# Infini-attention with MLP: inverse sums spread by four transfers, and head outputs weighed into the tile they arrive in

## The chip, the cores and the metric

The kernel runs on one core of one Trainium2 chip. The time is the device time of one execution in microseconds (us), and a kernel's time is the median of its runs. Five engines work side by side, each through its own queue of instructions: TensorE (PE in the profile; its weight loads are PEld), VectorE (DVE), ScalarE (ACT), GpSimd (POOL) and SyncE (SP). SP issues nearly all DMA transfers of the part that is spoken of here. "Granted clock" is the share of TensorE's full clock that the throttle allowed.

## The reference

A sequence of 2048 tokens of 1024 features goes through one pre-LayerNorm attention with a compressive memory, and then through one pre-LayerNorm MLP (1024 to 3584 to 1024), each with a residual. The attention has 32 heads of 32 features and works in four segments of 512 tokens. Cut to what the change touches:

```python
for s in range(N):                                   # 4 segments of 512 tokens
    qs, ks, vs = q[:, :, s], k[:, :, s], v[:, :, s]
    logits = jnp.einsum("bhqd,bhkd->bhqk", qs, ks) * scale + mask
    p = _softmax(logits, axis=-1)
    a_dot = jnp.einsum("bhqk,bhkd->bhqd", p, vs)
    pq = phi(qs)
    num = jnp.einsum("bhld,bhde->bhle", pq, M)
    den = jnp.einsum("bhld,bhd->bhl", pq, z)[..., None] + 1e-6
    a_mem = num / den
    o = g * a_mem + (1.0 - g) * a_dot
    outs.append(o)
    pk = phi(ks)
    M = M + jnp.einsum("bhld,bhle->bhde", pk, vs)
    z = z + jnp.einsum("bhld->bhd", pk)
...
return o @ wo
```

The kernel multiplies with unnormalised exponentials and puts the division by the softmax sum, and the factor `1 - g`, onto the outputs afterwards. One number for each head and token, the inverse sum times `1 - g`, therefore has to meet the 32 output features of that head, which lie on 32 partitions. Spreading that number over the 32 partitions is what the change is about.

## The kernel before

**Precision.** Each float32 matrix is split into a high part and a low part (`split`, lines 86 to 93: the high part is a cast on ACT or DVE, the low part a subtraction on DVE or POOL). One product takes three matmuls (`mm3`, lines 116 to 118: high by high, low by high, high by low).

**Halves and units.** The program works in two halves of 1024 tokens, which are two segments each. In a half, `attention` goes through eight groups `g` of four heads, and for each group through the half's two segments `sl`; a pair of group and segment is a unit, so a half has 16 units and the program 32. While the projections of one unit are computed (`dense`, from line 405: keys, queries, values), the four heads of the unit before are worked off in slots (`heads`, `slot`).

**Order.** The steps of a slot stand in one line of the program:

```python
PLAN = ('q1 r S2', 'q0 a0', 'q2 t0 w a1', 'q3 s0 o', 't1', 's1 t2')
```

q is a product of queries and keys with the reduction for the maximum behind it (`qk`, PE line 543, DVE line 544, ACT line 552), r the inverse of the sums (`inverse`, DVE line 559), w the spread (`weigh`), t the transposes of the probabilities (PE line 591, ACT line 593), s and S the subtraction that makes their low part (DVE line 598, tile `ptl`), a the products with the values (PE line 611, PSUM tile `po`), and o the output (`av_out`). The order of instructions on each engine, and the places of the transfers in SP's queue, follow from a scheduler that takes this program with its dependencies and its buffers.

**The spread.** For the last of a unit's four heads, `weigh` transposes the 16 columns of inverse sums (four heads by four blocks of 128 tokens), copies them into a corner of the tile `w`, stores that corner to a small DRAM tile (`r_dram`, line 575) and loads it back (line 576) so that each head's row of 512 numbers lands on 32 partitions. `w` is one quarter of a scratch tile, `sch` or `scl` in turn; only in the last unit of each half it is a tile of its own, `w`.

**The output.** `av_out` collects the four heads' results in the tile `ot`, of which there is one buffer: ACT copies the part from the low half of the probabilities (line 616), DVE adds the other part (line 622). After the fourth head POOL multiplies `ot` by `w` in place (line 624) and, but for the first segment, adds the memory's part `omt` (line 626). `ot` is then stored to `o_dram` (line 628), or, for the last group of heads, split on the spot into `oh` (ACT) and `ol` (DVE).

**The half end.** The out-projection of the half's first segment (`wo_first`, PSUM tile `pwo`) begins under the last two units. It needs the outputs of all groups: `load_o` (lines 702 to 710) loads them back from `o_dram` into `orr` and splits them into `oh` and `ol`. It also needs the weights `wo`, loaded as `wr` (line 719) and split into `wh` and `wl`; those of the fourth block go into tiles `zh` and `zl`, which take the buffers of `sch` and `scl`. So `zl` can be written only when no reader of `scl` is left.

## Time and profile before

| | |
|---|---|
| median of the runs | 2320.21 us |
| lowest and highest of 3 runs | 2318.26 and 2320.6 us |
| the profiled execution, its own time | 2317.62 us |
| its span, first to last instruction | 2315.8 us |
| mean granted clock over the span | 0.998 |
| bytes moved by DMA | 363.98 MB, mean 157 GB/s |

How to read the lines of the profile further on: a row of a stretch such as `100.00:470.00` names the stretch in us from the span's start, its length, the busy time of PE, PEld, DVE, ACT and POOL with the number of instructions in brackets, then the granted clock, the mean busy share of the 16 DMA engines, and GB/s. A row of a timeline gives the start, the duration, the engine, the source line, the operation and `out<-in`; the square bracket at its end is the idle time of that engine just before, and what ended it. A row of PE's waits names the waiting line, the releaser, the idle time in us, how often, and the longest.

The costs of the two steps that the change touches, over all 32 units, are seen in these rows (the groups of POOL's lines, then the answer for line 624 with what ended POOL's idle time ahead of it):

```profile
L626 POOL TENSOR_TENSOR ot<-ot,omt 128x512 f32<-128x512 f32 x24 | 31.0, 1292 | 1.8
```

```profile
L624 POOL TENSOR_TENSOR ot<-ot,scl x16: 1270/1293/1302, 82.6 to 1401.8; 128x512 f32<-128x512 f32 x16
L624 POOL TENSOR_TENSOR ot<-ot,sch x14: 1281/1287/1299, 114.2 to 1366.8; 128x512 f32<-128x512 f32 x14
L624 POOL TENSOR_TENSOR ot<-ot,w x2: 1291/1293/1295, 558.2 to 1439.2; 128x512 f32<-128x512 f32 x2
...
  DVE ot L622: 50.0, 28
  DVE mx L544: 8.8, 1
  DMA w<-r_dram: 4.0, 2
```

The product takes 1.29 us (the three numbers are the shortest, the median and the longest in ns). In 28 of its 32 occurrences POOL had waited for DVE's sum in `ot`, and in two, the last units of the halves, for the spread itself.

### The profile page before, as it was taken

What the parts mean: (1) busy time and instruction counts of PE and PEld (TensorE: products, weight loads), DVE (VectorE), ACT (ScalarE), POOL (GpSimd) and SP (SyncE); (2) the same over time, 40 slices, a digit from 0 to 9 for tenths busy, and PEclk for the clock granted to TensorE, in tenths of its full rate; (3) what the DMA queues carried; (4) which work ended last, traced back from release to release, by engine and by line L of the source; (5) the groups of instructions that cost most, each with busy time, mean ns of one, the idle gap of its engine ahead of it and who ended that gap; (6) DMA issues with size and microseconds to landing.
All of it is one profiled execution on the core that took longest, in us unless ns stands there. A gap on an engine that the chain in (4) does not pass through costs nothing.

```text
span 2315.8 us, 34768 instructions
## 1 busy us (share of the span) xinstructions
PE 2276.5 (98%) x11801; PEld 1897.0 (82%) x11801; DVE 1523.8 (66%) x3045; ACT 1226.5 (53%) x2581; POOL 827.9 (36%) x686
## 2 busy tenths in 40 slices
PE   8999999999999999999999998999999999999999
PEld 6888888877888888888888876788887888888887
DVE  6777777776655565777777776574566666477663
ACT  6777777774463445777777775363344223322321
POOL 4222222224244442233232223244445654155430
PEclk9999999999999999999999999999999999999999
DMA  6433333344466654433333343466567976476762
GB/s 180 109 94 95 99 101 95 94 138 152 144 210 176 182 168 139 118 101 95 94 94 97 94 118 114 163 204 192 157 191 260 346 242 223 149 257 216 257 233 92
DMA packets 327963, 363.98 MB, mean 157 GB/s; under 512 B 26830, under 2 KB 219882, under 8 KB 327786
## 3 DMA queue, kind: packets, MB, share of 16 engines
q1 hardware_dynamic: 264618, 325.06, 46.1%
q10 hardware_dynamic: 63168, 36.71, 5.3%
q8 instruction: 93, 1.52, 0.3%
q14 instruction: 84, 0.69, 0.1%
HBM read 234.98 MB, written 76.35 MB: 134 GB/s over the span
## 4 chain that ended last, share of the span: by engine, by line
PE 87%; DMA 4%; ACT 3%; DVE 3%; POOL 2%; issue 1%; SPq 0%; POOLq 0%; DVEq 0%; ACTq 0%
PE po L1297 23%; PE bps L901 10%; PE cps L901 7%; PE dps L901 6%; PE po L611 6%; PE ppt L591 5%; PE pqk L543 3%; PE vps L116 2%; PE vps L117 2%; PE vps L118 2%; PE qps L116 2%; PE qps L117 2%; PE qps L118 2%; PE kps L116 2%; PE kps L117 2%; PE kps L118 2%
## 5 line engine op out<-in xcount | busy, mean ns | idle before, releaser
L552 ACT ACTIVATE pr<-pr,mx 128x256 f32<-128x256 f32 (+3 forms) x512 | 287.1, 561 | 160.3 <-DVE mx L544 154.9
L544 DVE CUSTOM_DVE_ANT_0 pr<-pqk,mask 128x256 f32<-128x256 f32 (+3 forms) x512 | 244.4, 486 | 105.9 <-PE pqk L543 104.6
L598 DVE TENSOR_TENSOR ptl<-ppt,pth 128x512 fp32r<-128x512 f32 (+1 forms) x384 | 227.2, 599 | 95.6 <-ACT pth L593 93.4
L591 PE MATMUL ppt<-ident,pr 128*128 128x128 f32 x1280 | 222.9, 277 | 0.8 <-DVE ptl L598 0.6
L593 ACT CAST pth<-ppt 128x512 fp32r<-128x512 f32 (+1 forms) x384 | 193.9, 516 | 42.4 <-PE ppt L591 36.0
L93 POOL TENSOR_TENSOR wl<-wr,wh 128x1024 fp32r<-128x1024 f32 x52 | 124.6, 2397 | 230.4 <-PE pqk L543 103.0
L1307 DVE TENSOR_TENSOR c<-c,po 128x512 f32<-128x512 f32 x160 | 105.3, 682 | 144.0 <-PE po L1297 141.3
L591 PEld LDWEIGHTS ppt<-ident,pr 128*128 128x128 f32 x1280 | 165.0, 141 | 30.3 <-DVE ptl L598 1.6
L543 PE MATMUL pqk<-ks,qs 96*128 96x256 f32 (+3 forms) x512 | 162.5, 318 | 0.0
L611 PE MATMUL po<-ptl,vs 128*64 128x512 f32 (+3 forms) x512 | 154.4, 311 | 3.8 <-DVE ptl L598 3.6
L611 PE MATMUL po<-pth,vs 128*64 128x512 f32 (+3 forms) x512 | 156.1, 327 | 0.1
L1297 PE MATMUL po<-w2h,zh 128*128 128x512 f32 x378 | 120.9, 389 | 0.0
L543 PEld LDWEIGHTS pqk<-ks,qs 96*128 96x128 f32 x512 | 96.8, 189 | 23.7 <-DVE mx L544 2.5
L1154 POOL TENSOR_TENSOR w2r<-w2r 128x512 f32<-128x512 f32 x54 | 86.8, 1618 | 70.6 <-DMA w2r<-in_B_w 69.1
L901 PE MATMUL bps<-zh,sb 128*128 128x512 f32 x336 | 111.0, 391 | 0.0
L901 PE MATMUL bps<-zh,sa 128*128 128x512 f32 x336 | 110.7, 390 | 0.0
L116 PE MATMUL kps<-yh,wh 128*128 128x512 f32 (+1 forms) x264 | 110.5, 418 | 0.0
L116 PE MATMUL vps<-yh,wh 128*128 128x512 f32 x256 | 109.4, 427 | 0.9 <-DVE MZ L500 0.9
L116 PE MATMUL qps<-yh,wh 128*128 128x512 f32 x256 | 106.8, 417 | 0.0
L1297 PE MATMUL po<-w2h,hl 128*128 128x512 f32 x322 | 102.9, 389 | 0.0
L117 PE MATMUL kps<-yl,wh 128*128 128x512 f32 (+1 forms) x264 | 102.6, 389 | 0.1
L118 PE MATMUL kps<-yh,wl 128*128 128x512 f32 (+1 forms) x264 | 102.3, 387 | 0.0
(249 smaller groups left out, 6551.1 us busy)
## 6 DMA issues: line engine op xcount, KB each, us to landing
hr<-h_dram SPq DMA_DIRECT2D x112, 448.0 KB
w2r<-in_B_w SPq DMA_DIRECT2D x122, 256.0 KB
r<-in_B_w SPq DMA_DIRECT2D x56, 512.0 KB
h_dram<-ht ACTq DMA_DIRECT2D x84, 256.0 KB
ks<-kh SPq DMA_DIRECT2D x256, 64.0 KB
qs<-qh SPq DMA_DIRECT2D x256, 64.0 KB
wr<-in_A_wo SPq DMA_DIRECT2D x32, 512.0 KB
wx<-in_B_w SPq DMA_DIRECT2D x56, 256.0 KB
```

The source lines that it names most:

```text
L116: nc.tensor.matmul(ps, ah, bh, start=first, stop=False)
L117: nc.tensor.matmul(ps, ah, bl, start=False, stop=False)
L118: acts["mm"] = nc.tensor.matmul(ps, al, bh, start=False, stop=last)
L543: nc.tensor.matmul(pqk[:, :n], u["qs"][j][:, i * P:(i + 1) * P], u["ks"][j][:, 0:n], start=True, stop=True)
L544: nc.vector.tensor_tensor_reduce(out=st["pr"][:, offs[i]:offs[i] + n], in0=pqk[:, :n], in1=mask[:, 512 - n:512], op0=ALU.add, op1=ALU.min, ...
L552: nc.scalar.activation(pi, pi, AF.Exp, bias=mx[:, i:i + 1], scale=-1.0, accum_out=mx[:, 4 + i:5 + i])
L591: nc.tensor.transpose(ppt[:, o:o + P], pr[:, offs[i] + jk * P:offs[i] + (jk + 1) * P], ident)
L593: acts["pth"] = n, nc.scalar.copy(pth[:, base:base + w], ppt[:, :w])
L598: nc.vector.tensor_tensor(o, x0, x1, op=ALU.subtract)
L611: nc.tensor.matmul(po[:, P * jk:], v, st[part][:, koff[jk]:koff[jk] + w], start=(jk, part) == (0, "pth"), stop=(jk, part) == (2, "ptl"))
L901: nc.tensor.matmul(ps, x_[:, c, :], y_[:, c, :], start=first and c == 0 and n == 0, stop=last and c == 3 and n == 2, skip_group_check=True)
L1297: nc.tensor.matmul(ps, x_[:, k], y_[k], start=opens and k == 0 and i == 0, stop=closes and k == self.KP - 1 and i == 2, skip_group_check=True)
```

## The change

The spread's one load, whose pattern has three dimensions (4 heads, 32 repetitions, 512 numbers), becomes four loads of 32 partitions each. POOL's product is written into `w` instead of `ot`, the sum with `omt` too, and the store or the split reads `w`:

```diff
             d = r_dram[n]
             nc.sync.dma_start(d, w[0:16, 0:P])
-            nc.sync.dma_start(w, bass.AP(tensor=d.tensor, offset=d.offset, ap=[[512, 4], [0, DH], [1, 512]]))
+            for k in range(4):
+                nc.sync.dma_start(w[32 * k:32 * k + 32, :],
+                                  bass.AP(tensor=d.tensor, offset=d.offset + 512 * k, ap=[[0, DH], [1, 512]]))
...
             if j == 3:
-                nc.gpsimd.tensor_tensor(ot, ot, u["w"], op=ALU.mult)
+                w = u["w"]
+                nc.gpsimd.tensor_tensor(w, ot, w, op=ALU.mult)
                 if u["omt"] is not None:
-                    nc.gpsimd.tensor_tensor(ot, ot, u["omt"], op=ALU.add)
+                    nc.gpsimd.tensor_tensor(w, w, u["omt"], op=ALU.add)
                 if u["g"] < NG - 1:
-                    nc.sync.dma_start(o_dram[u["s"]][u["g"]], ot)
+                    nc.sync.dma_start(o_dram[u["s"]][u["g"]], w)
                 else:
                     oh, ol = o_tiles(half, u["s"] % 2)
-                    split(None, ot, oh[:, NG - 1, :], ol[:, NG - 1, :], hi_eng="scalar", lo_eng="vector")
+                    split(None, w, oh[:, NG - 1, :], ol[:, NG - 1, :], hi_eng="scalar", lo_eng="vector")
```

SP issues 96 transfers more (32 units, three each). PE, DVE, ACT and POOL execute the same number of instructions as before. With the outputs in `w`, the tile `ot` has its last reader in the product, and `w`, which lies in `sch` or `scl` but for two units, has later readers than before: the store or the split, and the sum with `omt`. The scheduler answers with another order at the two half ends; in the steady units the order is the old one. Three of these places follow, with the waits of each instruction in square brackets (the semaphore's name tells the engine or the DMA queue that it waits for). The lines of the changed kernel are two or three higher from the diff on (591 becomes 593, 611 becomes 613), and numbers at the end of a tile's name differ between the two programs.

PE at the end of half 0, in the last unit but one. Before, the first products with `zl` stand right behind the transposes:

```order
L591 MATMUL ppt<-ident,pr 128x128
L117 MATMUL pwo<-zl_6610,oh_6218 128x512 [waits Pool_49]
L118 MATMUL pwo<-zh_6609,ol_6219 128x512
L543 MATMUL pqk<-ks,qs 128x256 [waits DMAHW5_49,DMAHW4_49,DMAHW3_49]
L116 MATMUL pwo<-wh,oh_6218 128x512
L117 MATMUL pwo<-wl,oh_6218 128x512
L118 MATMUL pwo<-wh,ol_6219 128x512
L543 MATMUL pqk<-ks,qs 128x128 [waits DVE_49]
L611 MATMUL po<-pth,vs 64x512 [waits Activation_49]
L611 MATMUL po<-ptl,vs 64x512
L611 MATMUL po<-pth,vs 64x384 [waits Activation_49]
```

The same piece now:

```order
L593 MATMUL ppt<-ident,pr 128x128
L543 MATMUL pqk<-ks,qs 128x256 [waits DMAHW7_49,DMAHW6_49,DMAHW5_49]
L116 MATMUL pwo<-wh,oh_6257 128x512
L117 MATMUL pwo<-wl,oh_6257 128x512
L118 MATMUL pwo<-wh,ol_6258 128x512
L543 MATMUL pqk<-ks,qs 128x128 [waits DVE_49]
L613 MATMUL po<-pth,vs 64x512 [waits Activation_49]
L613 MATMUL po<-ptl,vs 64x512
L117 MATMUL pwo<-zl_6652,oh_6257 128x512 [waits Pool_49]
L118 MATMUL pwo<-zh_6651,ol_6258 128x512
L613 MATMUL po<-pth,vs 64x384 [waits Activation_49]
```

Seven matmuls have moved ahead of the first product that waits for `zl`. On DVE at that place, DVE's piece of `zl` has moved from ahead of `ol` to two operations behind it.

DVE in half 1, where the projections of the last unit begin (`kl` is the low part of its keys) and an output of an earlier group is loaded back (`orr`) and split. Before:

```order
L544 ISA mx 128x1
L93 TENSOR_TENSOR wl<-wr,wh 128x1024 [waits DMAHW6_49,Activation_49]
L705 CAST oh_15936<-orr 128x512 [waits DMAHW7_49]
L417 TENSOR_TENSOR kl<-kps,kh 128x512 [waits DMAHW2_49,DMAHW1_49,Activation_49]
L544 ISA pr,mx<-pqk,mask 128x384 [waits PE_49]
```

And now:

```order
L544 ISA mx 128x1
L93 TENSOR_TENSOR wl<-wr,wh 128x1024 [waits Activation_49]
L417 TENSOR_TENSOR kl<-kps,kh 128x512 [waits DMAHW1_49,DMAHW6_49,DMAHW0_49,Activation_49]
L708 CAST oh_16023<-orr 128x512 [waits DMAHW1_49]
L544 ISA pr,mx<-pqk,mask 128x384 [waits PE_49]
```

`kl` has moved ahead of the cast that waits for the load of `orr`.

POOL at the end of half 1, in the last unit but one. Before:

```order
L710 TENSOR_TENSOR ol_15937<-orr,oh_15936 128x512 [waits DMAHW6_49,DVE_49]
L624 TENSOR_TENSOR ot<-ot,scl 128x512 [waits DMAHW2_49,DMAHW1_49,DVE_49]
L93 TENSOR_TENSOR zl_16341<-wr,zh_16340 128x1024 [waits DMAHW5_49,DMAHW0_49,Pool_49]
L626 TENSOR_TENSOR ot<-ot,omt 128x512
L710 TENSOR_TENSOR ol_16678<-orr,oh_16677 128x512 [waits DMAHW2_49,PE_49,Activation_49]
```

And now:

```order
L713 TENSOR_TENSOR ol_16024<-orr,oh_16023 128x512 [waits DMAHW0_49,DVE_49]
L627 TENSOR_TENSOR scl<-ot,scl 128x512 [waits DMAHW4_49,DMAHW5_49,DMAHW3_49,DMAHW6_49,DMAHW2_49,DVE_49]
L629 TENSOR_TENSOR scl<-scl,omt 128x512 [waits Pool_49]
L93 TENSOR_TENSOR zl_16431<-wr,zh_16430 128x1024 [waits DMAHW7_49,DVE_49]
L713 TENSOR_TENSOR ol_16771<-orr,oh_16770 128x512 [waits DMAHW7_49,PE_49,Activation_49]
```

POOL's `zl` has moved behind the sum with `omt`, and it waits for DVE (the reader of the outputs in `scl`) where it waited for POOL.

## The prediction

> **What bounds the kernel now.** I read the page's busy line first, then the waits of PE, then busy time by stretches, and only then single instructions at the places which these point to.

> ```profile
> PE 2276.5 (98%) x11801; PEld 1897.0 (82%) x11801; DVE 1523.8 (66%) x3045; ACT 1226.5 (53%) x2581; POOL 827.9 (36%) x686
> ...
> PE pwo L117 <- POOL zl L93: 8.8, 2, 4.7
> PE pwo L117 <- POOL wl L93: 2.8, 2, 1.8
> PE pmm L398 <- DVE kl L417: 1.9, 1, 1.9
> ```

> ```profile
> 100.00:470.00 370.00, 369.32 (x2264) 313.65 (x2262) 268.99 (x767) 269.35 (x695) 95.60 (x102) 1.00 0.37 95
> 470.00:600.00 130.00, 120.98 (x634) 98.86 (x633) 87.63 (x180) 73.58 (x153) 47.48 (x42) 0.97 0.48 155
> ...
> 1340.00:1480.00 140.00, 127.94 (x680) 104.25 (x679) 93.88 (x203) 80.88 (x171) 46.66 (x39) 0.99 0.46 143
> ```

> PE is the bound. In steady attention (100 to 470 us) it is idle for 0.7 of 370 us, so nothing that happens to the spread or to the output tile there can gain time; it could only lose some. The two half ends, where the first out-projection begins, hold 9.0 and 12.1 us of PE idle time. The change can earn only there, at most some 21 us plus what a lowered clock costs after long gaps:

> ```profile
> 526.00:529.00 3.00, 3.00 (x9) 2.15 (x9) 0.80 (x5) 0.74 (x4) 0.00 (x0) 0.50 0.65 244
> ...
> 1363.60:1367.00 3.40, 3.40 (x27) 3.09 (x27) 2.79 (x8) 1.76 (x4) 0.90 (x2) 1.00 0.59 169
> ```

> The granted clock is the column after the five engines. PE waits 4.1 us until 523.64, and at 526 to 529 the clock is still 0.50; after the wait of 1.9 us that ends at 1363.6 it is 1.00.

> **The spread itself, 32 times.**

> ```profile
> 987.16 0.60 SPq L576 DMA_DIRECT2D sch<-r_dram  x1
> 989.36 1.17 SPq L380 DMA_DIRECT2D ks<-kh  x2
> ...
> 261.00:262.00 1.00, 1.00 (x8) 0.82 (x7) 1.00 (x5) 0.22 (x1) 0.00 (x0) 1.00 0.25 96
> ```

> In a stretch where the spread alone is on the DMA engines, their mean share is 0.25: it runs on 4 of 16, at 96 GB/s, so its 256 KB take 2.7 us. A transfer of 32 partitions should use all 16 (the 64 KB stacks have that shape); at the same 24 GB/s for each engine the four need 0.7 us together. Against that stand three more issues on SP: 0.59 us each (half of the 1.17) and a small gap, 1.9 us more. The data then land about 1 us earlier than now, and what is queued behind no longer waits on four busy engines. In steady units SP stands idle after the spread; the shortest room that I found is 2.2 us from its issue to the next one, where four issues take 2.5: ks loads 0.3 us late in a few units, under PE work of a whole unit. Cost there: 0. If that cover were gone, 0.3 us for each such unit.

> **A, half 0 (487 to 498).**

> ```profile
> 491.47 2.40 POOL L93 TENSOR_TENSOR wl<-wr,wh 128x1024 fp32r<-128x1024 f32 x1 [0.68 <-ACT wh L92]
> 493.83 0.67 DVE L710 TENSOR_TENSOR ol<-orr,oh 128x512 fp32r<-128x512 f32 x1
> 497.90 1.29 POOL L710 TENSOR_TENSOR ol<-orr,oh 128x512 fp32r<-128x512 f32 x1 [2.24 <-DVE oh L705]
> 498.21 0.33 PE L611 MATMUL po<-ptl,vs 128*64 128x256 f32 x1 [0.78 <-DVE ptl L598]
> ```

> The output tile is free sooner, so the scheduler puts the copy into ot earlier on ACT, and on POOL an ol of 1.29 ahead of wl. If that lets ACT go on sooner, the 0.78 goes away. But wl then runs some 1.4 later, from about 492.9 to 495.3, over the time in which DVE wants to do its own ol (493.83), and the two hold one another off (next part); DVE would wait about 1.4 there, with ptl and PE behind it, in place of the 0.78. I take half of the difference, **+0.3**, between -0.8 and +1.4.

> **B, last unit but one of half 0 (518 to 529).**

> ```profile
> 518.85 1.28 POOL L624 TENSOR_TENSOR ot<-ot,scl 128x512 f32<-128x512 f32 x1 [2.05 <-DVE ot L622]
> 519.14 0.38 PE L591 MATMUL ppt<-ident,pr 128*128 128x128 f32 x2
> 520.16 0.62 ACT L92 CAST oh<-ot 128x512 fp32r<-128x512 f32 x1 [2.23 <-POOL ot L624]
> 520.16 1.23 DVE L93 TENSOR_TENSOR zl<-wr,zh 128x1024 fp32r<-128x1024 f32 x1 [0.66 <-POOL ot L624]
> 520.21 3.38 POOL L93 TENSOR_TENSOR zl<-wr,zh 128x1024 fp32r<-128x1024 f32 x1
> 521.30 2.83 DVE L93 TENSOR_TENSOR ol<-ot,oh 128x512 fp32r<-128x512 f32 x1
> 523.64 0.80 PE L117 MATMUL pwo<-zl,oh 128*128 128x512 f32 x1 [4.12 <-POOL zl L93]
> ...
> 530.45 0.23 PE pwo L116
> ```

> zl lies in the buffer of scl. So far it waits for one reader of scl, the product on POOL; now the outputs stand in scl, and zl waits for ACT's cast and DVE's ol too. The rows also show POOL and DVE excluding one another: a product of this size takes POOL 2.40 alone (wl above), and zl here 3.38 behind DVE's 1.23; DVE's ol takes 2.83 while POOL works, 0.67 above. New order: product to 520.13, cast to 520.8, ol to 521.5, POOL's zl to 523.9. PE meets zl 0.3 later, but the changed order puts seven matmuls ahead of it, five of 512 columns at 0.23 and two short ones, 1.35 together. Gain 1.1. If DVE's own zl piece (1.23) gets in first, POOL ends at 525.1 and it is +0.2; lower bound -2.6 (a rival below). I take **-1.1**.

> **D, half 1, the start of the last unit's projections (1357 to 1364).**

> ```profile
> 1357.31 0.42 SPq L702 DMA_DIRECT2D orr<-o_dram  x1
> ...
> 1360.98 0.56 ACT L416 CAST kh<-kps 128x512 fp32r<-128x512 f32 x1
> 1362.52 0.43 DVE L705 CAST oh<-orr 128x512 fp32r<-128x512 f32 x1 [1.16 <-DMA orr<-o_dram]
> 1362.87 0.68 DVE L417 TENSOR_TENSOR kl<-kps,kh 128x512 fp32r<-128x512 f32 x1
> 1363.61 0.33 PE L398 MATMUL pmm<-vs,pkh 128*128 128x128 f32 x1 [1.93 <-DVE kl L417]
> ```

> The load orr is stuck behind the spread, DVE waits for it with kl queued behind, and PE waits for kl. Now kl stands ahead of that cast: it can start at 1361.55, when kh is done, not 1362.87, and PE gains 1.3. The load is issued 1.9 later, but on free engines, and lands about when it did. If it lands 1.9 later, DVE is held at that cast after kl instead, the work behind it is late for PE, and the gain goes: 0. The other bound is the whole wait, -1.9; I take **-1.3**.

> **E, the same unit of half 1 (1400 to 1411).**

> ```profile
> 1400.17 0.68 DVE L622 TENSOR_TENSOR ot<-po,ot 32x512 f32<-32x512 f32 x1
> 1401.53 0.39 PE L611 MATMUL po<-pth,vs 128*64 128x512 f32 x1
> 1401.82 1.27 POOL L624 TENSOR_TENSOR ot<-ot,scl 128x512 f32<-128x512 f32 x1 [8.80 <-DVE mx L544]
> 1403.17 3.38 POOL L93 TENSOR_TENSOR zl<-wr,zh 128x1024 fp32r<-128x1024 f32 x1
> 1406.51 1.27 POOL L626 TENSOR_TENSOR ot<-ot,omt 128x512 f32<-128x512 f32 x1
> 1406.60 0.59 PE L117 MATMUL pwo<-zl,oh 128*128 128x512 f32 x1 [4.68 <-POOL zl L93]
> ```

> Here zl passes behind the sum with omt as well. The product starts 1 us after ot is ready, which I put down to the spread's landing (the releaser named had long been done). With the spread earlier: product 1400.9 to 1402.2, sum to 1403.55, cast to 1404.2, ol to 1404.95, DVE's zl to 1406.1, POOL's to 1408.4. That is 1.8 later for zl, while PE has 2.0 to 2.2 us of moved work ahead of it (two products of 384 columns, one of 512, three pwo, one pqk, four transposes, two short ones). The low clock then lasts longer too, so I take **0**; if the product still starts at 1401.82, +1.0; bounds -0.5 to +1.0.

> **C and F, the last unit of each half.**

> ```profile
> 556.86 0.68 DVE L622 TENSOR_TENSOR ot<-po,ot 32x512 f32<-32x512 f32 x1
> 558.16 1.29 POOL L624 TENSOR_TENSOR ot<-ot,w 128x512 f32<-128x512 f32 x1 [1.88 <-DMA w<-r_dram]
> ...
> 1437.70 0.68 DVE L622 TENSOR_TENSOR ot<-po,ot 32x512 f32<-32x512 f32 x1
> 1439.23 1.29 POOL L624 TENSOR_TENSOR ot<-ot,w 128x512 f32<-128x512 f32 x1 [2.11 <-DMA w<-r_dram]
> 1441.83 0.62 ACT L707 CAST oh<-orr 128x512 fp32r<-128x512 f32 x1 [4.51 <-DMA orr<-o_dram]
> ```

> Nothing covers the spread here: POOL waits for it, and from there one chain of latency (cast, ol, LayerNorm, loads of wo) reaches PE, which waits for wl at its end: 2.8 us in the two halves. A spread 1 us earlier lets the product start when ot is ready (557.54 and 1438.38), 0.6 earlier in half 0 and 0.85 in half 1. In half 1 the orr load bounds the next cast: ACT waits 4.5 for it. It is now issued ahead of a wo load that stood before it, and off the crowded engines, so I let this step gain another 0.35. The wo load that moves back is cast by ACT only after w is; if it is late then, half 0 loses 0.5. **-0.6 and -1.2**; bounds +0.5 and -1.0, 0 and -1.8.

> **Sum.** +0.3 - 1.1 - 0.6 - 1.3 + 0 - 1.2 = -3.9. The profiled execution took 2317.62 us (span 2315.8), 2.6 below the median of 2320.21: 2313.7 for such a profile, **2316.3** in the runs.

> **Rivals.** (1) The gap at B is now about 3.0 us, between 1.9 (clock kept) and 4.1 (halved). If the clock is kept, some 5.4 us at half speed (523.6 to 529) vanish, of which 1.5 counts before PE meets DVE's ptl; if A's stall goes too (1.1 better than taken) and D gives its whole 1.9: -7.1, 2313.1. [...] (2) The four transfers are no faster: their rate is that of reading one DRAM row over and over, or SP's issues are the limit. Then C and F give 0, D -0.6, E +1.0: -0.4, 2319.8. The share of 0.25 speaks against it. [...] (3) Slower: zl waits for the new readers and the moved matmuls don't cover it, because they stop for ptl or for a PSUM bank themselves. At E zl then ends at 1409.4 (product at 1401.82, DVE's piece first), +2.85, at B at 525.1, +1.5, and the longer gaps add about 1.5 at half clock: +5.9 there, beside -2.8 from A, C, D and F: +3.1, 2323.3. It decides once less than about 1 us of moved work runs before zl. The rows before show ptl and the banks ready at both places, which speaks against it.

> **How the numbers follow.** 0.2% (4.6 us) is about what can be told from no change. Forecast 0.45 (half of it beyond 4.6 below: 0.23 faster, 0.22 the same), rival 1 0.23 (faster), rival 2 0.12 (same), rival 3 0.20 (0.06 same, 0.14 slower). Faster 0.46, same 0.40, slower 0.14. The range 2310.5 to 2323.0 takes in rivals 1 and 2 and most of 3; the forecast alone has 2313 to 2319.

> **What would show it.** A DMA share well above 0.25 during the spreads, and POOL's waits for w below 1 us, show the transfers right. PE's wait for kl near 1362 gone: D. PE's wait for zl about 3 us near 521 and 4 to 5 near 1404, with POOL's zl released by DVE's ol: B and E. Steady stretches must stay without idle time; new PE waits there, or for pqk on a DMA, would make the forecast wrong, and so would zl waits above 5 us at both places.

## The result, and the profile after

The changed kernel takes 2313.46 us (median of 10 runs, 2310.76 to 2315.82) against 2321.16 us before (10 runs): a ratio of 0.9966, 95% interval 0.9956 to 0.9976, or 7.7 us less. Run again in a later set it took 2314.45 us against 2320.55, a ratio of 0.9975 (0.9965 to 0.9984), 6.1 us less. The forecast was 3.9 us less, with 2316.3 as its time. The sign and the range were right, and most of the places; the size was half of the first of these figures and two thirds of the second.

The page of the changed kernel has the same busy share of PE, 98%.

PE's waits (total, how often, longest), the changed kernel:

```profile
PE pwo L117 <- POOL zl L93: 7.8, 2, 4.7
PE po L613 <- DVE ptl L600: 4.1, 3, 1.5
...
PE pwo L117 <- POOL wl L93: 1.5, 1, 1.5
...
PE pmm L398 <- DVE kl L417: 0.6, 1, 0.6
```

The wait for `kl` fell from 1.9 to 0.6, that for `zl` from 8.8 to 7.8, that for `wl` from 2.8 to 1.5. In a second pair of profiles (below) the first two fall again, from 1.9 to 0.6 and from 10.8 to 7.4; the wait for `wl` is 2.4 in both, so its fall is not clear of variation.

Busy time by stretches, the changed kernel (same columns as before):

```profile
470.00:600.00 130.00, 122.61 (x647) 100.73 (x647) 90.11 (x183) 75.03 (x153) 47.05 (x42) 0.99 0.48 155
960.00:1340.00 380.00, 380.00 (x2332) 323.08 (x2331) 280.92 (x807) 282.65 (x725) 112.46 (x112) 1.00 0.37 95
```

PE's idle time between 470 and 600 us fell from 9.0 to 7.4 us. The row from 960 to 1340 is the interesting one: PE is busy for all of it, as it was before, and yet this stretch became shorter. That is seen in the starts of the same instruction, the 18th and the 31st copy into `vt` on ACT. Before:

```profile
948.45 0.59 ACT L464 COPY vt<-vps 128x512 f32<-128x512 f32 x1
```

```profile
1349.73 0.59 ACT L464 COPY vt<-vps 128x512 f32<-128x512 f32 x1
```

And after:

```profile
946.42 0.59 ACT L464 COPY vt<-vps 128x512 f32<-128x512 f32 x1
```

```profile
1346.45 0.59 ACT L464 COPY vt<-vps 128x512 f32<-128x512 f32 x1
```

It is 401.28 us from one to the other before, and 400.03 after. All profiles of this study can be cut at such marks. The table has the lengths in us of three stretches: half 0's end (15th copy into `vt` to the 8th sum `hb`, the first operation behind the half's out-projection and residual), the steady units of half 1 (as above), and half 1's end (31st copy to 16th `hb`). The last columns are the number of stretches of 3.41 us at half clock in the two half ends, and the median of all runs with the ratio to the runs of before in the same set. The stretches are from one profiled execution each, which need not be one of median length.

| kernel | spread | outputs in | half 0's end | steady, half 1 | half 1's end | at half clock | median, ratio (95%) |
|---|---|---|---|---|---|---|---|
| before | 1 | ot | 158.0 | 401.28 | 159.8 | 3 | 2321.16 |
| before, second profile | 1 | ot | 158.4 | 401.22 | 163.0 | 4 | 2320.01, 1.0001 (0.9991 to 1.0011) |
| after | 4 | w | 155.3 | 400.03 | 158.5 | 2 | 2313.46, 0.9966 (0.9956 to 0.9976) |
| after, second profile | 4 | w | 154.6 | 399.99 | 158.6 | 1 | 2314.45, 0.9975 (0.9965 to 0.9984) |
| four transfers only | 4 | ot | 157.6 | 401.35 | 157.8 | 3 | 2314.37, 0.9972 (0.996 to 0.9983) |
| outputs in w only | 1 | w | 156.0 | 400.11 | 163.1 | 5 | 2316.68, 0.9986 (0.9977 to 0.9994) |
| last group in ot | 4 | w, ot | 157.9 | 400.00 | 156.2 | 3 | 2313.4, 0.9974 (0.9963 to 0.9984) |
| zl on DVE | 4 | w | 157.6 | 399.96 | 153.7 | 2 | 2310.47, 0.996 (0.9947 to 0.9974) |
| own tile | 4 | w | 155.2 | 399.99 | 153.5 | 2 | 2306.82, 0.9947 (0.9934 to 0.9959) |
| own tile, again | 4 | w | 153.1 | 399.97 | 153.5 | 0 | 2305.4, 0.9936 (0.9924 to 0.9948) |
| own tile, zl on DVE | 4 | w | 155.3 | 400.01 | 155.2 | 1 | 2308.68, 0.9951 (0.9938 to 0.9963) |
| own tile, one transfer | 1 | w | 156.2 | 399.95 | 162.5 | 4 | 2317.6, 0.9985 (0.9976 to 0.9994) |
| own tile, two transfers | 2 | w | 166.8 | 399.93 | 168.4 | 8 | 2333.4, 1.0059 (1.0046 to 1.0072) |
| before, own tile | 1 | ot | 154.9 | 401.45 | 163.1 | 3 | 2321.03, 1.0004 (0.9995 to 1.0013) |

The other parts of the program (the opening, the steady units of half 0, the stretch between the halves, the MLP) have the same instructions in all of them; the MLP took 804.2 to 808.6 us without any order by kernel, so a difference of a few us there, such as the 2.1 between the first two profiles, is variation between executions. Fourteen profiles agree far better at the steady units: 399.9 to 400.1 us wherever outputs go into `w`, 401.2 to 401.5 wherever they stay in `ot`.

### The profile page after: what moved, and what is told of

It reads as the page before. It is cut to its first block, busy times and chain, and to the rows that moved or that the text cites. A ratio compares the mean times of both kernels' runs of the same rounds, so it can differ in the third digit from the quotient of the medians.

```text
span 2309.1 us, 34959 instructions
## 1 busy us (share of the span) xinstructions
PE 2273.1 (98%) x11801; PEld 1895.7 (82%) x11801; DVE 1519.7 (66%) x3045; ACT 1227.7 (53%) x2581; POOL 830.6 (36%) x686
## 4 chain that ended last, share of the span: by engine, by line
PE 69%; DMA 1%; POOL 1%; ACT 1%; DVE 1%; issue 1%; SPq 0%; POOLq 0%; ACTq 0%; DVEq 0%
PE po L1300 23%; PE bps L904 10%; PE cps L904 7%; PE dps L904 6%; PE po L613 3%; PE ppt L593 3%; PE pqk L543 2%; PE vps L116 1%; PE vps L117 1%; PE vps L118 1%; PE kps L116 1%; PE kps L117 1%; PE qps L117 1%; PE qps L116 1%; PE kps L118 1%; PE qps L118 1%
## 5 line engine op out<-in xcount | busy, mean ns | idle before, releaser
L544 DVE CUSTOM_DVE_ANT_0 pr<-pqk,mask 128x256 f32<-128x256 f32 (+3 forms) x512 | 244.5, 486 | 107.1 <-PE pqk L543 105.9
L93 POOL TENSOR_TENSOR wl<-wr,wh 128x1024 fp32r<-128x1024 f32 x52 | 124.8, 2399 | 229.5 <-PE pqk L543 128.0
L613 PE MATMUL po<-pth,vs 128*64 128x512 f32 (+3 forms) x512 | 156.0, 327 | 0.0
L116 PE MATMUL vps<-yh,wh 128*128 128x512 f32 x256 | 109.4, 427 | 0.9 <-DVE MZ L500 0.9
L116 PE MATMUL kps<-yh,wh 128*128 128x512 f32 (+1 forms) x264 | 110.0, 417 | 0.0
L116 PE MATMUL qps<-yh,wh 128*128 128x512 f32 x256 | 106.9, 418 | 0.0
L117 PE MATMUL kps<-yl,wh 128*128 128x512 f32 (+1 forms) x264 | 102.3, 388 | 0.1
```

The lines of the kernel that those rows point to most:

```text
L116: nc.tensor.matmul(ps, ah, bh, start=first, stop=False)
L117: nc.tensor.matmul(ps, ah, bl, start=False, stop=False)
L544: nc.vector.tensor_tensor_reduce(out=st["pr"][:, offs[i]:offs[i] + n], in0=pqk[:, :n], in1=mask[:, 512 - n:512], op0=ALU.add, op1=ALU.min, ...
L613: nc.tensor.matmul(po[:, P * jk:], v, st[part][:, koff[jk]:koff[jk] + w], start=(jk, part) == (0, "pth"), stop=(jk, part) == (2, "ptl"))
```

## The experiments

### The two halves of the change apart

The four transfers alone:

```diff
-                nc.gpsimd.tensor_tensor(w, ot, w, op=ALU.mult)
+                nc.gpsimd.tensor_tensor(ot, ot, u["w"], op=ALU.mult)
...
```

> Leaves out the second half of the change: four transfers, outputs still weighed in place in ot. Theory (the gain is made at the two half ends alone, place by place): D gains about 1.0 (PE's wait for kl falls from 1.9 to 0.6), the last units of the halves gain 0.7 and 0.6 because the spread lands earlier, the place of the zl wait in half 0 stays as before (4.1 us of wait, 6.8 us at half clock), so about -2.3 against before: 2318.9. Rival (the faster transfers also relieve the steady units or the MLP): -5 or more, 2316 or less, with the lead over before growing in 100 to 470 us and 960 to 1340 us.

Measured: 2314.37, 6.2 less than the runs of before in the same set. The wait for `kl` fell to 0.6 as expected, and the wait for `zl` in half 0 stayed at 4.1. What was not expected stands in half 1. POOL there, in the last unit but one (start, duration, operation, idle time before it), the four transfers alone:

```profile
1401.28 1.29 POOL L626 TENSOR_TENSOR ot<-ot,scl 128x512 f32<-128x512 f32 x1 [7.92 <-DVE ot L624]
1402.65 2.34 POOL L93 TENSOR_TENSOR zl<-wr,zh 128x1024 fp32r<-128x1024 f32 x1
```

and PE, same kernel and place:

```profile
1405.05 0.50 PE L117 MATMUL pwo<-zl,oh 128*128 128x512 f32 x1 [2.53 <-POOL zl L93]
```

The product now starts when `ot` is ready, and PE waits 2.53 us for `zl` where it waited 4.68. Neither the steady units of half 0 nor those of half 1 (401.35) became shorter, so the rival's reason is out although its number came nearer. The theory was worked out on the first profile of before, and against that the three stretches of the table gained 2.4 us; against the second profile they gained 5.9.

The outputs in `w` alone, with the one transfer:

```diff
-            for k in range(4):
-                nc.sync.dma_start(w[32 * k:32 * k + 32, :],
-                                  bass.AP(tensor=d.tensor, offset=d.offset + 512 * k, ap=[[0, DH], [1, 512]]))
+            nc.sync.dma_start(w, bass.AP(tensor=d.tensor, offset=d.offset, ap=[[512, 4], [0, DH], [1, 512]]))
```

> Leaves out the first half of the change: one transfer as before, outputs weighed into the spread tile. Theory: the changed order at the last unit but one of half 0 gains 2.1 (wait for zl 3.1 instead of 4.1, half clock 3.4 us instead of 6.8), the half 1 unit loses 0.4 to 0.9 since the product there still waits for the late spread, wl in half 0 loses 0.1; about -1.4 against before: 2319.8. Rival (the free ot relieves the steady units): -4 or more, 2317 or less.

Measured: 2316.68, 3.9 less. Half 0's end gained 2.0 to 2.3 as the theory has it; half 1's end, at 163.1, is no shorter than in either profile of before. The theory missed the steady units of half 1, 1.2 us shorter. What released ACT's copies into `ot` after an idle time (total, times), before:

```profile
L616 ACT COPY ot<-po x128: 574/577/583, 57.0 to 1436.7; 32x512 f32<-32x512 f32 x128
...
  DMA o_dram<-ot: 5.5, 13
  PE po L611: 2.0, 2
```

and in the changed kernel:

```profile
L618 ACT COPY ot<-po x128: 575/578/583, 56.3 to 1432.7; 32x512 f32<-32x512 f32 x128
...
  PE po L613: 4.1, 3
```

Thirteen times ACT stood still until the store of the one buffer `ot` had landed, 5.5 us in all, once in a group of heads, behind the store of one of its two units. With the outputs in `w` that wait is gone, and with the four transfers alone it is there (5.6 us, 13 times). Seven of the thirteen lie in half 1, and at each of these seven the changed kernel gets ahead by 0.17 to 0.20 us; those in half 0 cost PE nothing, and why is not shown. On PE it never showed as idle time, of which that stretch has none before or after, but in longer matmuls: those of queries and keys took 319 ns in the mean there before, and 315 after. One of them, 5 us after the wait of ACT that ended at 969.84, took 0.44 us instead of 0.34; the steps from the one to the other were not traced.

The two halves do not add up. Alone they take off 6.2 and 3.9 us, together 6.1 to 7.7. On top of the four transfers the outputs in `w` are worth 0 to 0.9 us in the medians (2314.37 against 2314.45 and 2313.46): in the profiles they gain 1.3 us in the steady units of half 1 and 2.3 to 2.9 in half 0's end, and lose 0.7 to 0.9 in half 1's end, but the two profiled executions of the changed kernel were 2.3 and 3.6 us under its medians.

### How much is variation between executions

Both kernels once more:

> The kernel before, unchanged, for a second profile of it. Theory (what the profile of the change gained in the opening, the steady units of half 1 and the MLP, 2.7 us in all, is variation between executions): same median within 2 us, and its lead over the first profile moves by 1 us or more in at least one of those stretches. Rival (those gains are made by the change): the two profiles agree within 0.3 us in each of those stretches.

> The changed kernel once more, for a second profile of it. Theory: the leads at the half ends come again within 0.3 us each (zl place of half 0 +2.1, D +1.0, last units +0.7 and +0.6, zl place of half 1 -0.4), those elsewhere do not. Rival: all come again. Time 2313.5 within 2 us by both.

Measured: 2320.01 and 2314.45. The second profile of before agrees with the first within 0.3 us in the opening and in the steady units, and its MLP is 0.7 shorter; the theory's 1 us was not reached there. It is the half end that moved: 163.0 us instead of 159.8 with the same instructions. Some 1.6 us of it arise at 1372 to 1379 us, where ACT waits 3.32 us for the load of an earlier output instead of 0.77, and PE in the end 1.97 us for `ptl` instead of 0.62. The rest arises at the spread of the last unit but one. SP at that place, before, first profile:

```profile
1394.33 0.32 SPq L575 DMA_DIRECT2D r_dram<-scl  x1
1395.69 0.59 SPq L576 DMA_DIRECT2D scl<-r_dram  x1
```

and the second:

```profile
1396.45 0.32 SPq L575 DMA_DIRECT2D r_dram<-scl  x1
1399.88 0.59 SPq L576 DMA_DIRECT2D scl<-r_dram  x1
```

The spread can be issued only when the small store has landed, and from one issue to the other it was 1.36 us in one profile and 3.43 in the other. In the second, PE waited 6.7 us for `zl` instead of 4.7, and two stretches ran at half clock there instead of one. Of the five profiles with one transfer, four have 162.5 to 163.1 us for this half end, though not by the same waits (with the outputs in `w` alone the small store took 1.36 us too): the profile that the prediction was made from is the odd one. The granted clock says the same for all runs: its mean was 0.9962 over 60 runs of before and 0.9979 over 20 of the changed kernel, while the first profile of before had 0.998. That is 2 x 0.0038 x 2318 = 18 us at half clock in a run of before, some five stretches, against 10 us, three stretches, after. At most half of that time is lost, so up to 4 us of the 6.1 to 7.7 are clock, by this estimate. At one and the same granted clock, 0.998, four runs of before took 2317.6 us in the mean and ten of the changed kernel 2313.6, so that some 4 us are there without it.

The half ends of the changed kernel came again as expected (154.6 and 158.6), and so did the steady units of half 1, which the theory had put down to variation; there the rival was right.

### The place where zl is waited for

Three kernels loosen the wait for `zl` in different ways. In the first, the last group of heads keeps its outputs in `ot`, so that `zl` waits only for the product:

```diff
-                w = u["w"]
-                nc.gpsimd.tensor_tensor(w, ot, w, op=ALU.mult)
+                w = u["w"] if u["g"] < NG - 1 else ot
+                nc.gpsimd.tensor_tensor(w, ot, u["w"], op=ALU.mult)
```

> The change, but in the last group of heads the outputs stay in ot, so that zl waits for the product alone again. Theory (zl's new readers cost where the spread is early enough; the free ot gains in the steady units of half 1; the early spread gains at kl): half 0 has the old wait for zl, 4.1 us, and two lowered windows, 2 us worse than the change there; half 1 has a wait of 2.5 us as with the four transfers alone, 2 us better; ACT's waits for the store of ot stay at 0 in the steady units, lead of 1.2 us there. Sum: as the change, 2314 within 2 us. Rival (the order at the zl place of half 0 is the main part of the gain): 2316.5 or more.

Measured: 2313.4. All three parts came as the theory has them: half 0's end back to 157.9, half 1's end 156.2, steady units 400.00. PE's wait for `zl` was 4.11 in half 0 and 2.59 in half 1. So the new readers of `scl` cost what they were expected to cost in half 1, about 2 us, and the order that they forced gains as much in half 0; in the sum it makes no difference.

In the second, the low parts of `wo`'s fourth and fifth block change engines:

```diff
-            wts[0, k] = wo_halves(wo_raw(0, k), k, wo_home() if k < 3 else [x_[:, 0:2] for x_ in more])
+            wts[0, k] = wo_halves(wo_raw(0, k), k, wo_home() if k < 3 else [x_[:, 0:2] for x_ in more],
+                                  "vector" if k == 3 else None)
...
-        wts[1, 0] = wo_halves(wo_raw(1, 0), 0, [x_[:, 2:4] for x_ in more])
+        wts[1, 0] = wo_halves(wo_raw(1, 0), 0, [x_[:, 2:4] for x_ in more], "gpsimd")
```

> The change, with the low part of wo's fourth block made by DVE (1.23 us alone) and that of the fifth by POOL, the other way round than now. Theory (POOL's 2.3 to 3.4 us for zl stand in the wait): the waits for zl fall by 1.1 in half 0 and by 2.2 in half 1, one or two lowered windows fewer: -4 against the change, 2310. Rival (DVE is the engine on which everything else there waits, so zl's 1.2 us push the probabilities' low parts back by as much): within 1 us of the change.

Measured: 2310.47, ratio 0.996. PE's two waits for `zl` are 3.7 us together instead of 7.8, and half 1's end is 4.8 us shorter. In half 0 the gain was more than eaten up: its end is 2.3 to 2.9 us longer than with the change. PE waits 1.31 us for `pth` and then 2.06 for `zl` there, and two stretches run at half clock, where the change has one or none. So the time came as forecast, but not from the parts that it was made of; that is luck.

In the third, both units of the last group have a spread tile of their own, and `zl` is free of them:

```diff
-            w = u["w"] = tmp("w") if u["g"] == NG - 1 and u["s"] % 2 else scr[n][:, 1]
+            w = u["w"] = tmp("w") if u["g"] == NG - 1 else scr[n][:, 1]
```

> The change, with a spread tile of its own in both units of the last group, so that zl waits for no reader of the last units' outputs. Theory: PE's waits for zl (7.4 to 7.8 us in two places) fall below 1 us each, and with them two lowered windows of 3.4 us; behind them PE waits for ol of the last group instead, which I put at half of that: -5 against the change, 2309. Rival (the wait for ol or for the product takes the whole place of the wait for zl): within 1 us of the change, 2313 to 2315.

Measured: 2306.82, ratio 0.9947 (0.9934 to 0.9959); the best version of the study, and faster than both kernels. PE's waits with it:

```profile
PE po L613 <- DVE ptl L600: 4.5, 4, 1.5
PE pwo L117 <- POOL wl L93: 2.7, 2, 1.5
PE po L613 <- ACT pth L595: 1.3, 1, 1.3
PE pwo L117 <- POOL zl L93: 1.1, 2, 0.8
```

`zl` is down from 7.8 to 1.1 us, and nothing of that size took its place.

Both of these edits together:

> Both of the two before: a spread tile of its own for the last group, and DVE and POOL exchanged for the two low parts. Theory: no better than the tile alone (2309), since zl is ready early there whoever makes it. Rival (the two gains add): 2306 or less.

Measured: 2308.68. No better than the tile alone, as the theory has it.

### The spread in the best version

Here the product is bound by the spread alone, so the spread can be measured. The kernel with its own tile again, with one transfer (the edit is that of the outputs in `w` alone), and with two:

```diff
-            for k in range(4):
-                nc.sync.dma_start(w[32 * k:32 * k + 32, :],
-                                  bass.AP(tensor=d.tensor, offset=d.offset + 512 * k, ap=[[0, DH], [1, 512]]))
+            for k in range(2):
+                nc.sync.dma_start(w[64 * k:64 * k + 64, :],
+                                  bass.AP(tensor=d.tensor, offset=d.offset + 1024 * k, ap=[[512, 2], [0, DH], [1, 512]]))
```

> The kernel with a spread tile of its own in both units of the last group, once more, on the chip and beside the runs of the next three. 2307 within 2 us by every theory; the product in the last unit but one of half 1 starts about 3.4 us after the first issue of the spread.

> The same, with the spread as one transfer. Theory (with zl off the spread, the four transfers are worth only the place of kl and the last units): 1.0 + 0.7 + 0.6 and half a lowered window more, about +3, 2310; from the spread's issue to the product in the last unit but one of half 1 6.1 us, as in every profile with one transfer. Rival (the four transfers gain in the steady units too): 2312 or more.

> The same, with the spread as two transfers of 64 partitions, whose outermost dimension has 2 entries. Theory (a transfer of this kind runs on as many DMA engines as its outermost dimension has entries, 4 for the one transfer and more for those of 32 partitions): no faster than one transfer, 6.1 us or more from issue to product, and a DMA share of at most 0.25 while the spread is alone; 2310 or more. Rival (what counts is the number of transfers under way): half way, about 4.8 us, and a share of 0.3 to 0.5; 2308.5.

Measured: 2305.4, 2317.6 and 2333.4. The spread's issue on SP and the product on POOL, last unit but one of half 1, with four transfers:

```profile
1391.82 1.72 SPq L577 DMA_DIRECT2D w<-r_dram  x4
```

```profile
1395.43 1.29 POOL L627 TENSOR_TENSOR w<-ot,w 128x512 f32<-128x512 f32 x1 [8.64 <-DMA w<-r_dram]
```

with one:

```profile
1397.44 0.59 SPq L576 DMA_DIRECT2D w<-r_dram  x1
```

```profile
1403.41 1.27 POOL L625 TENSOR_TENSOR w<-ot,w 128x512 f32<-128x512 f32 x1 [11.16 <-DMA w<-r_dram]
```

with two:

```profile
1412.68 1.14 SPq L577 DMA_DIRECT2D w<-r_dram  x2
```

```profile
1421.01 1.26 POOL L627 TENSOR_TENSOR w<-ot,w 128x512 f32<-128x512 f32 x1 [13.40 <-DMA w<-r_dram]
```

From the first issue to the product it is 3.61 us with four transfers, 5.97 with one and 8.33 with two. Two are slower than one, so it isn't the number of transfers under way that counts. A stretch in which the two are alone on the DMA engines (the last two columns are the share of 16 engines and GB/s):

```profile
1418.00:1419.00 1.00, 1.00 (x6) 0.83 (x6) 0.00 (x0) 0.00 (x0) 0.00 (x0) 1.00 0.13 49
```

0.13 is two engines of 16 for both transfers together, at half the rate of the one transfer's four (49 GB/s against 96). The outermost dimension of the pattern has 2 entries here, 4 in the one transfer and 32 in the four. So the shares of 0.13 and 0.25 are as many engines as the pattern has entries, as the theory has it; with 32 entries it was 0.52 (the changed kernel near 260 us, further on).

On the time the theory fell: it gave the four transfers 3 us here, and with them the kernel is 12 us faster. The rival's number was nearer, but not for its reason, since the steady units are as long with one transfer as with four (399.95 and 399.97). What happens is seen on DVE with the one transfer:

```profile
1406.70 0.69 DVE L93 TENSOR_TENSOR ol<-w,oh 128x512 fp32r<-128x512 f32 x1 [4.71 <-ACT oh L92]
1407.31 0.42 DVE L598 TENSOR_TENSOR ptl<-ppt,pth 128x256 fp32r<-128x256 f32 x1
```

and on PE:

```profile
1407.78 0.47 PE L611 MATMUL po<-ptl,vs 128*64 128x256 f32 x1 [3.76 <-DVE ptl L598]
```

DVE stands 4.71 us at `ol`, which needs the weighed outputs and so the spread; the low part of the probabilities, `ptl`, is queued behind it, and PE waits for that. `zl` is long done. The late spread reaches PE by another queue. The order has a part in this: with one transfer the scheduler has put `ol` ahead of this piece of `ptl`, and with four two reductions behind it:

```profile
1395.06 0.42 DVE L600 TENSOR_TENSOR ptl<-ppt,pth 128x256 fp32r<-128x256 f32 x1
...
1398.77 0.69 DVE L93 TENSOR_TENSOR ol<-w,oh 128x512 fp32r<-128x512 f32 x1 [1.68 <-ACT oh L92]
```

So the 9.0 us of half 1's end (162.5 against 153.5) are those of the faster spread together with the order that the scheduler makes of it, and no kernel here separates the two. In half 0's end PE, DVE, ACT and POOL have the same order in both kernels, and there the four transfers alone gain 1.0 to 3.1 us.

The same edit on the kernel before, neither half of the change made:

> The kernel before, neither half of the change made, with a spread tile of its own in both units of the last group. Theory (most of what can be had at the half ends is zl's wait): the waits for zl, 8.8 to 10.8 us, fall below 1 us each, two to three lowered windows fewer, ACT's waits for the store of ot (5.5 us) stay: -8 against before, 2312. Rival (without the early spread and the free ot, oh and ol of the last group come late and PE waits there instead): -3 or less, 2317 or more.

Measured: 2321.03, ratio 1.0004. The theory fell and the rival held: PE's waits for `zl` did fall to 1.1 us, and those for `ptl` and `pth` rose, from 3.6 and none before, to 7.6 and 2.7:

```profile
PE po L611 <- DVE ptl L598: 7.6, 5, 3.6
PE po L611 <- ACT pth L593: 2.7, 1, 2.7
...
PE pwo L117 <- POOL zl L93: 1.1, 2, 0.8
```

Half 0's end became 3.1 us shorter all the same (154.9 against 158.0); half 1's end, at 163.1, did not, and DVE stands 4.53 us at an `ol` ahead of `ptl` there as in the kernel just shown. In half 1 `zl` was the place where the late spread came to light, and not its cause. The profiled execution was 3.6 us under the median, so its stretches flatter this kernel. The tile of its own is worth nothing with one transfer (2321.03 against 2321.15; with the outputs in `w` 2317.6 against 2316.68), and 7 to 9 us on top of the change (2313.46 and 2314.45 against 2306.82 and 2305.4).

## Why the prediction was right in its sign and short in its size

**What bounds the kernel, and where it can earn.** Right for the half ends. Wrong in one sentence: that nothing which happens to the output tile in steady attention can gain time, since PE is idle there for 0.7 of 370 us. The output tile gained 1.2 to 1.3 us in the steady units of half 1, by taking away ACT's 13 waits for the store (5.5 us). The stretch that the sentence names, 100 to 470 us, lies in half 0 and gained nothing indeed; half 1 was taken to be the same. ACT's waits for the store stood in the profile of before (the rows of line 616 above) and were put at nothing because PE did not stand still, but idle time on PE is not all that a late engine costs it.

**The spread.** More than four engines work on it now, as forecast. In the steady unit near 260 us, with the four transfers alone, the changed kernel has twice the share of 0.25:

```profile
260.00:261.00 1.00, 1.00 (x7) 0.82 (x7) 0.96 (x4) 0.00 (x0) 0.00 (x0) 1.00 0.52 144
```

That a transfer of 32 partitions spreads wide could be seen before on the stacks of 64 KB (one of them alone):

```profile
110.10:110.40 0.30, 0.30 (x6) 0.30 (x5) 0.00 (x0) 0.30 (x2) 0.30 (x1) 1.00 0.85 191
```

But 191 GB/s at a share of 0.85 is 14 GB/s for each busy engine, where 24 were taken. The four do not take the 0.7 us that were put down for all 16 engines: 256 KB at 144 GB/s take some 1.8 us, an estimate, about as long as SP issues them (1.72). "About 1 us earlier" was too little even so where it counts: it is 2.4 us (5.97 against 3.61) in the last unit but one, where other transfers run beside it. The cost in steady units was 0, as taken.

**A** was put at +0.3 and cost 0.1 (by the starts of the same instructions behind it), and PE waits 1.3 us for `ptl` there in place of the 0.8, as described. **D** was put at -1.3: PE's wait for `kl` fell by 1.3, in every profile with four transfers. **C** and **F** were put at -0.6 and -1.2; against the first profile of before the changed kernel gained 0.7 and 0.6 there in its first profile, 0.1 and 0.2 in its second.

**B** was put at -1.1; half 0's end as a whole, for which A, B and C make -1.4, gained 2.7 and 3.7 in the two pairs of profiles. The wait for `zl` is 3.13 us, as forecast (3.0):

```profile
521.04 2.34 POOL L93 TENSOR_TENSOR zl<-wr,zh 128x1024 fp32r<-128x1024 f32 x1 [1.46 <-DVE ol L93]
...
523.44 0.50 PE L117 MATMUL pwo<-zl,oh 128*128 128x512 f32 x1 [3.13 <-POOL zl L93]
```

and POOL got to `zl` ahead of DVE's piece, so that it took 2.34 where it took 3.38 behind that piece. What came on top is the clock, which I had left to the first rival: one lowered stretch instead of two in the first profile and none in the second. Half of that rival's mechanism is shown, but its 2313.1 is near the time by luck: D did not give its whole 1.9 nor did A's stall go, and a gap of about 3.0 does not decide whether the clock is kept. The gap of 3.13 us was followed by half clock in the first profile, and one of 3.1 us was not in the second (last section).

**E** was put at 0, as a later `zl` covered by moved work. The change waits 4.69 us there:

```profile
1401.13 3.38 POOL L93 TENSOR_TENSOR zl<-wr,zh 128x1024 fp32r<-128x1024 f32 x1 [1.46 <-DVE ol L93]
...
1404.57 0.69 PE L117 MATMUL pwo<-zl,oh 128*128 128x512 f32 x1 [4.69 <-POOL zl L93]
```

which is what it was before in the profile that I had (4.68), though `zl` ends 1.2 us later there, counted from the 31st copy into `vt`: the moved work did cover that much. It is 2.2 more than with the four transfers alone (2.53), and 2 less than in the second profile of before (6.7). So the 0 is made of a gain of some 2.2 us by the early spread and a loss of as much by the new readers.

**The sum.** In the first pair of profiles, which holds the execution that the sum of 3.9 was made from, the three stretches of the table gained 5.3 us. Half 0's end gained 2.7, where 1.4 was forecast (B is the term that was too small, by the clock); the steady units of half 1 gained 1.3, where nothing was put down; half 1's end gained 1.3, where D, E and F make 2.5 (F came at half its size, and two losses of some 0.2 each, one of them at E, stand against D). That the third error hid a good part of the other two is luck. In the second pair the gain is 9.3, since half 1's end took 163.0 us before and not 159.8: the terms there were taken from an execution that lacks some of the stalls which most runs of before have. How much of the median's 6.1 to 7.7 this makes stays open, because the profiled executions of the changed kernel are under their medians too.

Rivals 2 and 3 are out: the transfers are faster, and moved work did cover the later `zl` in half 1, while in half 0 the wait for it became shorter.

## What to carry to other kernels

Read what a wait is made of before taking its releaser away: here `zl`, `kl` and `ptl` were three queues through which one late transfer reached PE, and freeing `zl` alone moved the wait of half 1 to the next (0 us in the time), while the same edit was worth 7 to 9 us once the transfer was fast and the order had followed. When a transfer repeats one row over many partitions, give its pattern an outermost dimension of many entries (from issue to product it was 8.33 us with 2, 5.97 with 4 and 3.61 with 32 here), and check the DMA share while it runs alone (0.13 and 0.25 here for the first two). And before a sum is made from one profile, compare its granted clock with those of the runs: where they differ in the third digit (here 0.998 against 0.9962), the profile lacks some of the stalls that the median has.

## What the runs showed of the hardware that was not expected

```profile
1387.00:1390.30 3.30, 2.08 (x13) 1.60 (x14) 2.86 (x9) 2.77 (x8) 1.99 (x1) 1.00 0.08 9
1390.50:1393.60 3.10, 3.10 (x14) 2.45 (x13) 1.56 (x8) 0.53 (x3) 0.00 (x0) 0.50 0.85 254
520.00:523.30 3.30, 1.65 (x8) 1.17 (x8) 2.35 (x8) 2.56 (x8) 0.00 (x0) 1.00 0.56 225
523.50:526.70 3.20, 3.20 (x13) 2.72 (x12) 1.40 (x4) 1.77 (x4) 0.00 (x0) 0.50 0.02 5
```

PE was busy for 2.08 of 3.30 us and for 1.65 of 3.30, and the clock was halved in the stretch behind; windows as busy as these are the exception, as the count below shows. In the second profile of the changed kernel a wait of 3.1 us for `zl` fell across two windows:

```profile
519.10:522.40 3.30, 1.60 (x10) 0.98 (x8) 1.98 (x7) 2.37 (x6) 1.84 (x2) 1.00 0.00 0
522.50:525.80 3.30, 1.89 (x8) 1.27 (x9) 3.30 (x4) 0.22 (x2) 1.27 (x1) 1.00 0.24 56
```

Open too is why the small store's landing took 1.36 us in one execution and 3.43 in another of the same program; the traces show only that it did.
